# Attention and two gated products on one core: v for its norms loaded two squares ahead into buffers of its own, the fourth stage's results turned a quarter later

## The chip, the cores and the metric

The kernel runs on one core of a Trainium2 chip. A core has a matrix engine (TensorE, PE in the profile), a vector engine (DVE), a scalar engine (ACT), GpSimd (POOL), and SyncE (SP), which here issues all the large transfers; 16 DMA engines carry them. The metric is the device time of one execution in microseconds.

## What is computed

Float32 attention over 4 batches, 12 heads, 448 positions and 64 elements, whose result is 1792 rows of 768, and behind it two products in a chain (their weights come as float64):

```python
q_n, k_n = (rmsnorm(q, g_q), rmsnorm(k, g_k))
scores = scale * np.matmul(q_n, k_n.transpose(0, 1, 3, 2))
attn = np.exp(scores - max); attn = attn / (sum + 1e-09)
x = np.matmul(attn, v)               # then heads side by side: 1792 x 768
a = x @ w_a; b = x @ w_b             # 768 -> 1536
x = a * b @ w_out                    # 1536 -> 768
h = x @ w_in                         # 768 -> 2048
g = np.maximum(h, 0.0) + alpha * np.minimum(h, 0.0)
out = g @ w_out                      # 2048 -> 768
```

(The lines are shortened; the second product's weights are `moe2_w_in` and `moe2_w_out`.)

## The kernel before

Two streams of work are woven together by the code's order. The first is attention (`att_steps`): heads go in 24 pairs, six to a batch, and a pair in seven pieces of 64 queries of both heads; a step takes two pieces: scores `s` on TensorE, the maximum on DVE (L417), its scaling (L430) and the exponential (L434) on ACT, the probabilities as float16 high and low parts `p` on ACT and DVE (L479, L480), a transposing DMA `pT` on SP (L486), and after a pair's seven pieces the product with v (`x<-pT,v`). A pair is prepared ahead: `kr` and `qr` are loaded (L202, L206), squared for their norms (L232, L235), scaled, cast (L343, L341), transposed by DMA (`qT` L351, `kT` L354), and `qS`, qT with its halves exchanged, is copied from it (L357, L358). From batch 1 on TensorE's scores take qT first and qS after it.

The second stream is four matmul stages to a batch, `a`, `y`, `h` and `o`, in the order a0 y0 h0 o0 a1 y1 a2 h1 o1 y2 a3 h2 y3 o2 h3 o3. Each stage is a row of chains of matmuls into one of three PSUM buffers; between them the table `RATE` says how many attention steps are let in. On first use a piece of weights is loaded as raw float64 (L628), made float32 on ACT and DVE (L644, L647, L650), scaled and split to float16 parts `w` (L711, L712), used, and stored (L715, `sc_a` to `sc_o`); later batches load the stored parts (L624). So all conversion falls into a0 to o0, some 100 to 415 us.

Two places matter here. `vnorm(b, p)` squares v of a pair on ACT (L371) with the row sums in `ssv`; six of them are summed on TensorE by a matmul with ones (`tot<-ssv`) and give v's scale in a batch. Its buffer `vn` is loaded on the spot (L363), from a pool with two buffers, `ob`, that `finish` uses too. `stage_o` makes six chains of four quarters; `finish(m, ps)` takes a chain's result: ACT puts it from PSUM to `t` (L880), TensorE turns it in four transposes (L887), ACT scales it to `ob` (L889), SP stores it (L890). It is called behind the first quarter of the next chain, and for the last chain at once.

The code's order is a wish: a scheduler places each instruction in a queue for its engine by its own estimate, so that a small edit can change the order of many instructions behind it. Each engine then works through its queue in that order. The names in the rows are those of the program's tiles: `p<-g,w` is a matmul of stage o, `p<-x,w` of stage a.

Of the kernel before, what the change touches and what calls it, by code (L numbers as in the profile page):

```python
# [8 lines left out]
F32 = mybir.dt.float32  # L9
# [10 lines left out]
def attention_gated_mlps_kernel(  # L20
# [16 lines left out]
    B, H, S, D = q.shape  # L37
# [3 lines left out]
    NP = H // 2  # L41
    NI = S // 64
    KB = 4
    KP = S // KB
# [9 lines left out]
    ob_p = ctx.enter_context(tc.tile_pool(name="ob", bufs=2))  # L54
    in_p = ctx.enter_context(tc.tile_pool(name="in", bufs=2))
# [80 lines left out]
    def setup():  # L136
        for t, src in ((gT, g_q), (gkT, g_k)):
            for h in range(2):
                nc.sync.dma_start(
                    out=t[64 * h:64 * h + 64], in_=src.rearrange("(d o) -> d o", o=1)  # L140
                )
        make_identity(nc, ident)
        for t in qT0:
            nc.gpsimd.memset(t, 0.0)
        for t in stat:
            nc.gpsimd.memset(t, 1.0)

    def setup1():
        nc.gpsimd.tensor_tensor(gT, gT, gkT, op=ALU.mult)
        nc.gpsimd.tensor_scalar(gT, gT, float(D) ** -0.5, None, op0=ALU.mult)  # L150

    def setup0():
        nc.vector.memset(ones, 1.0)
        for t in p16:
            nc.vector.memset(t, 0.0)

    def setup2():
        nc.gpsimd.dma_start(out=gbc, in_=g_q.rearrange("(o d) -> o d", o=1).broadcast_to([128, D]))
        nc.gpsimd.dma_start(out=gkb, in_=g_k.rearrange("(o d) -> o d", o=1).broadcast_to([128, D]))
        nc.gpsimd.dma_start(out=al, in_=alpha.rearrange("(f p) -> p f", p=128))  # L160
# [35 lines left out]
    def load_qk(g):  # L196
        if g >= B * NP:
            return
        b, p = divmod(g, NP)
        qr = in_p.tile([128, NI, D], F32, tag="qr", name="qr")  # L200
        kr = in_p.tile([KP, 2 * KB, D], F32, tag="kr", name="kr")
        nc.sync.dma_start(  # L202
            out=kr.rearrange("p (h i) d -> p h i d", h=2),
            in_=k[b, 2 * p:2 * p + 2].rearrange("h (p i) d -> p h i d", i=KB),
        )
        nc.sync.dma_start(  # L206
            out=qr, in_=q[b, 2 * p:2 * p + 2].rearrange("h (p i) d -> (h p) i d", i=NI)
        )
        P[g]["qr"], P[g]["kr"] = qr, kr
# [15 lines left out]
    def prep0(g):  # L225
        if g >= B * NP:
            return
        d = P[g]
        st = stat[g // 2 % 2][:, g % 2]
        sq = one_p.tile([128, 2 * KB, D], F32, tag="sq", name="sq")[:, 0:NI]  # L230
        sk = one_p.tile([128, 2 * KB, D], F32, tag="sq", name="sk")[0:KP]
        i = nc.scalar.activation(out=sk, in_=d["kr"], func=AF.Square)  # L232
        if g in PIN1:
            tc.keep_in_program_order(i)
        nc.scalar.activation(out=sq, in_=d["qr"], func=AF.Square)  # L235
        i = nc.vector.reduce_sum(out=st[:KP, NI:NS], in_=sk, axis=AX.X)
        if g in PIN0:
            tc.keep_in_program_order(i)
        nc.vector.reduce_sum(out=st[:, 0:NI], in_=sq, axis=AX.X)
# [41 lines left out]
    def prep3f(g):  # L281
        prep3f_a(g)
        prep3f_b(g)
# [74 lines left out]
        nc.sync.dma_start(out=qS[64:128], in_=qT[0:64])  # L358
        d["qT"], d["kT"] = (qT, qS), kT

    def load_vn(b, p):
        vn = ob_p.tile([KP, 2, KB, D], F32, tag="ob", name="vn")
        nc.sync.dma_start(  # L363
            out=vn, in_=v[b, 2 * p:2 * p + 2].rearrange("h (p i) d -> p h i d", i=KB)
        )
        return vn

    def vnorm(b, p):
        vn = load_vn(b, p)
        sv = one_p.tile([128, 2 * KB, D], F32, tag="sq", name="sq")[0:KP]  # L370
        nc.scalar.activation(  # L371
            out=sv, in_=vn.rearrange("p h i d -> p (h i) d"), func=AF.Square,
            accum_out=ssv[:, b, p:p + 1],
        )

    def vscale(b):
        power(total(ssv[:, b], NP), sx[:, b:b + 1], ix[:, b:b + 1])
# [232 lines left out]
    for st in stages:  # L610
        n, parts, _ = CHAINS[st[0]]
# [128 lines left out]
    def next_w():  # L740
        u = cur[0]
        cur[0] += 1
        w16.pop(u)
        advance(u)
        if tasks:
            tasks.pop(0)()

    def unit():
        w = w16[cur[0]]
        return w.rearrange("p l (k f) -> p l k f", f=128)  # L750

    def prod(o, w, kk, x, first, last):
        hi, lo = w[:, 0, kk, :], w[:, 1, kk, :]
        mm(o, hi, x[:, 0], first, False)
        mm(o, hi, x[:, 1], False, False)
        mm(o, lo, x[:, 0], False, last)

    def new_ps():
        return ps_m.tile([128, 512], F32, tag="p", name="p")

    def tmp():
        return tmp_p.tile([128, S], F32, tag="t", name="t")
# [110 lines left out]
    def stage_o(b):  # L873
        NT, PT = 4, S // 4
        k = CHAINS["o"][2]

        def finish(m, ps):
            t = tmp()

            nc.scalar.activation(  # L880
                out=t.rearrange("q (p c) -> q c p", c=NI),
                in_=ps.rearrange("q (c p) -> q c p", c=NI),
                func=AF.Copy, scale=inv["o"][:, m:m + 1],
            )
            po = new_ps()[:PT].rearrange("p (t f) -> p t f", t=NT)
            for i in range(NT):
                nc.tensor.transpose(po[:, i, :], t[:, i * PT:(i + 1) * PT], ident)  # L887
            ob = ob_p.tile([PT, NT, 128], F32, tag="ob", name="ob")
            nc.scalar.activation(out=ob, in_=po, func=AF.Copy, scale=cum[:PT, b:b + 1])  # L889
            nc.sync.dma_start(  # L890
                out=out[b * S:(b + 1) * S, m * 128:(m + 1) * 128].rearrange("(t p) f -> p t f", t=NT),
                in_=ob,
            )

        c = cum[:, b:b + 1]
        nc.gpsimd.tensor_tensor(c, ix[:, b:b + 1], iab[:, b:b + 1], op=ALU.mult)
        nc.gpsimd.tensor_tensor(c, c, iy, op=ALU.mult)
        nc.gpsimd.tensor_tensor(c, c, icg, op=ALU.mult)
        nc.gpsimd.tensor_tensor(c, c, ix[:, b:b + 1], op=ALU.mult)
        late = None  # L900
        for m in range(KD):
            ps = new_ps()[:, 0:S]
            for part in range(4):
                yield
                hw = unit()
                for kk in range(k):
                    prod(
                        ps, hw, kk, G[b, part * k + kk],
                        part + kk == 0, part == 3 and kk == k - 1,
                    )  # L910
                if part == 0 and late:
                    finish(*late)
                next_w()
            late = (m, ps)
        finish(*late)
        for f in range(KF2):
            G.pop((b, f))
# [4 lines left out]
    if True:  # L922
        load_qk(0)
        setup()
        load_qk(1)
        setup0()
        prep0(0)
        setup1()
        prep3f(0)
        prep1((0,), NI, NS)  # L930
        prep2f(0)
        prep4f(0)
        prep0(1)
        prep1((0,), 0, NI)
        load_v(0)
        prep1((1,))
        load_v(1)
        load_qk(2)
        setup2()
        att = att_steps()  # L940
        n, done = 0, 0
        W0, EVERY = 4, 2
        while done < NP:
            g = [next(att) for _ in range(3)][-1]
            n += 1
            if n >= W0 and (n - W0) % EVERY == 0:
                advance((n - W0) // EVERY - 9 if n < 22 else -1)
            if n == 8:
                setup3()
                setup4()  # L950
            if g is not None:
                done += 1
        state["pin"] = False
        advance(-1)

        def step():
            nonlocal done
            done += next(att, None) is not None

        for i, st in enumerate(stages):  # L960
            s, b = st[0], int(st[1])
            if s == "a":
                while done < (b + 1) * NP:
                    step()
            n, parts, _ = CHAINS[s]
            ticks = n * parts
            gen = {"a": stage_a, "y": stage_y, "h": stage_h, "o": stage_o}[s](b)
            want, acc = 3 * RATE.get(st, 0), 0
            for _ in gen:
                acc += want  # L970
                while acc >= ticks:
                    acc -= ticks
                    step()
# [30 lines left out]
```

## Time and profile before

| | |
|---|---|
| median of 3 runs | 1224.51 us (1223.84 to 1224.89) |
| the profiled execution, and its span | 1225.36 us, 1223.6 us |
| mean granted TensorE clock | 0.985 |
| PE busy | 1158.7 us (95%) |
| ACT busy | 714.4 us (58%) |
| DVE busy | 673.7 us (55%) |
| POOL busy | 11.9 us (1%) |

The span is the time from the first to the last instruction that the profiler recorded on the core; the execution's time has a little around it. Shares are of the span. A busy share is a mean over stages that have different limits.

### The profile page before, as it was taken

What the parts mean: (1) busy time and instruction counts of PE and PEld (TensorE: products, weight loads), DVE (VectorE), ACT (ScalarE), POOL (GpSimd) and SP (SyncE); (2) the same over time, 40 slices, a digit from 0 to 9 for tenths busy, and PEclk for the clock granted to TensorE, in tenths of its full rate; (3) what the DMA queues carried; (4) which work ended last, traced back from release to release, by engine and by line L of the source; (5) the groups of instructions that cost most, each with busy time, mean ns of one, the idle gap of its engine ahead of it and who ended that gap; (6) DMA issues with size and microseconds to landing.
All of it is one profiled execution on the core that took longest, in us unless ns stands there. A gap on an engine that the chain in (4) does not pass through costs nothing.

```text
span 1223.6 us, 18095 instructions
## 1 busy us (share of the span) xinstructions
PE 1158.7 (95%) x6550; PEld 595.6 (49%) x6550; DVE 673.7 (55%) x1442; ACT 714.4 (58%) x1458; POOL 11.9 (1%) x32
## 2 busy tenths in 40 slices
PE   6997999889988899989999999999999999999998
PEld 3553554444434444445455445545555555554554
DVE  7898999999999767667542465332101440002400
ACT  7998999999999767675533465452111440113311
POOL 1000000000000000000000000000000000000000
PEclk9997999999999999999999999999999999999999
DMA  6558999999999999797854637876333333354343
GB/s 186 175 164 217 311 324 324 278 298 301 318 261 300 266 257 246 189 230 177 208 153 126 168 106 168 192 191 163 104 116 116 116 117 107 105 151 128 95 129 88
DMA packets 311241, 234.65 MB, mean 192 GB/s; under 512 B 175440, under 2 KB 284496, under 8 KB 311152
## 3 DMA queue, kind: packets, MB, share of 16 engines
q1 hardware_dynamic: 311040, 233.43, 71.8%
q8 instruction: 51, 0.84, 0.3%
q0 software_dynamic: 112, 0.07, 0.1%
q14 instruction: 38, 0.31, 0.1%
HBM read 155.79 MB, written 32.24 MB: 154 GB/s over the span
## 4 chain that ended last, share of the span: by engine, by line
PE 52%; DMA 1%; ACT 1%; DVE 1%; issue 0%; SPq 0%; ACTq 0%
PE p L108 48%; PE s L108 2%; PE x L108 2%; PE p L887 1%; DMA pT<-p 1%; DMA kr<-in_k_dram 0%; ACT t L880 0%; DMA qT<-q 0%; ACT pf L434 0%; ACT p L479 0%; DVE p L480 0%; DVE nm L417 0%; SPq L486 0%; DVE ab L788 0%; ACT x L530 0%
## 5 line engine op out<-in xcount | busy, mean ns | idle before, releaser
L108 PEld LDWEIGHTS <-w 128*128 128x128 f16 x4896 | 474.9, 99 | 466.9 <-issue 39.9
L108 PE MATMUL p<-x,w 128*128 128x448 f16 x1728 | 336.6, 354 | 0.3 <-DVE ab L788 0.2
L108 PE MATMUL p<-g,w 128*128 128x448 f16 x1152 | 228.1, 354 | 6.3 <-ACT g L847 2.2
L108 PE MATMUL p<-y,w 128*128 128x448 f16 x1152 | 222.3, 353 | 0.2 <-DVE t L862 0.2
L108 PE MATMUL p<-ab,w 128*128 128x448 f16 x864 | 169.5, 356 | 1.4 <-ACT ab L766 1.2
L417 DVE TENSOR_REDUCE nm<-s 128x2 f32<-128x896 f32 x84 | 91.2, 1085 | 38.3 <-PE s L108 38.2
L480 DVE SCALAR_TENSOR_TENSOR p<-pf,ri,p 128x448 f16<-128x448 f32 x126 | 84.1, 680 | 30.7 <-ACT p L479 30.5
L479 ACT ACTIVATE p<-pf,ri 128x448 f16<-128x448 f32 x126 | 81.2, 664 | 33.9 <-DMA pT<-p 25.8
L862 DVE SCALAR_TENSOR_TENSOR t<-t,al,p 128x448 f32<-128x448 f32 x55 | 37.3, 678 | 100.6 <-ACT t L861 100.5
L434 ACT ACTIVATE pf<-s,nm,esc 128x448 f32<-128x448 f32 x126 | 90.1, 719 | 1.4
L788 DVE SCALAR_TENSOR_TENSOR ab<-p,inv_a,t 128x448 f32<-128x448 f32 x48 | 32.5, 678 | 100.0 <-PE p L108 99.8
L880 ACT ACTIVATE t<-p,inv_o 128x448 f32<-128x448 f32 x24 | 25.6, 1065 | 81.5 <-PE p L108 81.5
L712 DVE SCALAR_TENSOR_TENSOR w<-wf,sc,w 128x768 f16<-128x768 f32 (+1 forms) x76 | 70.1, 928 | 3.0 <-ACT w L711 2.5
L791 ACT ACTIVATE junk<-ab 128x448 bf16<-128x448 f32 x48 | 27.6, 575 | 70.4 <-DVE ab L788 69.8
L711 ACT ACTIVATE w<-wf,sc 128x768 f16<-128x768 f32 (+1 forms) x76 | 65.5, 869 | 3.4 <-DMA sc_h<-w 1.7
L644 ACT ACTIVATE wf<-raw 128x768 f32<-128x768 f32 (+1 forms) x76 | 63.7, 843 | 4.6 <-DMA raw<-in_moe_w_in_dram 2.7
L650 DVE SCALAR_TENSOR_TENSOR wf<-raw,wf 128x768 int32<-128x768 int32 (+1 forms) x76 | 65.8, 867 | 0.3
L658 ACT ACTIVATE junk<-wf 128x768 bf16<-128x768 f32 (+1 forms) x76 | 59.2, 779 | 1.4 <-DVE wf L650 1.3
L861 ACT ACTIVATE t<-p 128x448 f32<-128x448 f32 x55 | 29.8, 542 | 48.0 <-PE p L108 47.9
L108 PE MATMUL s<-kT,qT 128*64 128x448 f16 x252 | 48.4, 376 | 9.2 <-DMA kT<-k 6.3
L847 ACT ACTIVATE g<-t,cgf 128x448 f16<-128x448 f32 x55 | 36.7, 668 | 34.6 <-DVE t L862 34.6
L848 DVE SCALAR_TENSOR_TENSOR g<-t,cgf,g 128x448 f16<-128x448 f32 x55 | 37.5, 682 | 29.5 <-ACT g L847 29.5
(137 smaller groups left out, 1030.5 us busy)
## 6 DMA issues: line engine op xcount, KB each, us to landing
w<-sc_a SPq DMA_DIRECT2D x72, 384.0 KB, 3.2
w<-sc_h SPq DMA_DIRECT2D x48, 384.0 KB, 3.1
w<-sc_o SPq DMA_DIRECT2D x72, 256.0 KB, 3.1
w<-sc_y SPq DMA_DIRECT2D x36, 384.0 KB, 3.2
raw<-in_moe_w_in_dram SPq DMA_DIRECT2D x16, 768.0 KB, 7.8
raw<-in_moe_w_out_dram SPq DMA_DIRECT2D x24, 512.0 KB, 6.3
raw<-in_moe_w_a_dram SPq DMA_DIRECT2D x12, 768.0 KB, 7.2
raw<-in_moe_w_b_dram SPq DMA_DIRECT2D x12, 768.0 KB, 6.4
```

Source lines behind the costliest of these rows:

```text
L108: nc.tensor.matmul(out=o, lhsT=a, rhs=b, start=first, stop=last)
L417: nc.vector.tensor_reduce(out=nm, in_=ps[:, :, 0:S], axis=AX.X, op=ALU.max, negate=True)
L434: nc.scalar.activation(out=pf, in_=ps[:, j, 0:S], func=AF.Exp, bias=nm[:, j:j + 1], scale=scale[j], accum_out=su[:, j:j + 1],)
L479: nc.scalar.activation(out=t[:, 0, :, 0:KP], in_=pf, func=AF.Copy, scale=r)
L480: nc.vector.scalar_tensor_tensor(out=t[:, 1, :, 0:KP], in0=pf, scalar=r, in1=t[:, 0, :, 0:KP], op0=ALU.mult, op1=ALU.subtract,)
L644: nc.scalar.activation(out=t, in_=hi.bitcast(F32), func=AF.Prelu, scale=2.0 ** -112, alpha=-(2.0 ** 32))
L650: nc.vector.scalar_tensor_tensor(out=ti, in0=lo, scalar=29, in1=ti, op0=ALU.logical_shift_right, op1=ALU.bitwise_or)
L658: nc.scalar.activation(out=junk(768, size(kind)), in_=t, func=AF.Square, accum_out=sums[0][:, j:j + 1])
L711: nc.scalar.activation(out=w[:, 0], in_=t, func=AF.Copy, scale=s)
L712: nc.vector.scalar_tensor_tensor(out=w[:, 1], in0=t, scalar=s, in1=w[:, 0], op0=ALU.mult, op1=ALU.subtract)
L848: nc.vector.scalar_tensor_tensor(out=x[:, 1], in0=t, scalar=cgf[:, f:f + 1], in1=x[:, 0], op0=ALU.mult, op1=ALU.subtract,)
L862: nc.vector.scalar_tensor_tensor(out=t, in0=t, scalar=al[:, f:f + 1], in1=ps, op0=ALU.mult, op1=ALU.add)
```

## The change

`vn` gets two buffers of its own in another pool (tag `vn` of `in_p`). The loads for the first two squares are issued at the end of the setup, and `vnorm` for pair n issues the load for pair n + 2 behind its square. In `stage_o` a chain's `finish` is called behind the second quarter of the next chain instead of the first.

```diff
-    def load_vn(b, p):
-        vn = ob_p.tile([KP, 2, KB, D], F32, tag="ob", name="vn")
+    vns = {}
+
+    def load_vn(n):
+        if n >= B * NP:
+            return
+        b, p = divmod(n, NP)
+        vns[n] = vn = in_p.tile([KP, 2, KB, D], F32, tag="vn", name="vn")
         nc.sync.dma_start(
             out=vn, in_=v[b, 2 * p:2 * p + 2].rearrange("h (p i) d -> p h i d", i=KB)
         )
-        return vn
 
     def vnorm(b, p):
-        vn = load_vn(b, p)
+        n = b * NP + p
+        vn = vns.pop(n)
...
             accum_out=ssv[:, b, p:p + 1],
         )
+        load_vn(n + 2)
...
-                if part == 0 and late:
+                if part == 1 and late:
                     finish(*late)
...
         load_qk(2)
+        load_vn(0)
+        load_vn(1)
         setup2()
```

Behind these lines the line numbers of the changed kernel are 5 to 8 higher: its L880 is L886, L711 is L717, L479 is L485, L371 is L376; L202 to L358 keep theirs. The scheduler's order stays the same on ACT, DVE and PE for the first 235 to 265 us and changes at many places from there to about 490 us. Three of them follow.

ACT at the end of o0, from the last preparation of a pair to the first attention step behind o0, before the change:

```order
L235 ACTIVATE sq<-qr 128x448
L530 ACTIVATE x_5_5165<-x 128x448
L385 ACTIVATE v_5486<-vr,sx 112x8x64
L232 ACTIVATE sk<-kr 112x512
L880 ACTIVATE t<-p,inv_o 128x7x64
L479 ACTIVATE p_0_108<-pf,ri 128x4x112
L889 ACTIVATE ob<-p,cum 112x512
L479 ACTIVATE p_1_109<-pf,ri 128x4x112
L235 ACTIVATE sq<-qr 128x448
L430 ACTIVATE nm<-nm,esc 128x2
```

The same place on ACT after the change, where L886 and L895 are the same two steps of `finish`:

```order
L235 ACTIVATE sq<-qr 128x448
L536 ACTIVATE x_5_5169<-x 128x448
L391 ACTIVATE v_5490<-vr,sx 112x8x64
L886 ACTIVATE t<-p,inv_o 128x7x64
L485 ACTIVATE p_0_108<-pf,ri 128x4x112
L895 ACTIVATE ob<-p,cum 112x512
L485 ACTIVATE p_1_109<-pf,ri 128x4x112
L232 ACTIVATE sk<-kr 112x512
L436 ACTIVATE nm<-nm,esc 128x2
```

The t of the last chain (L880, L886) now stands ahead of L232, the square of a kr, and no longer behind it.

ACT around the t of the fifth chain of o0 (`w_4971` to `w_5063` are the last pieces of o0's weights), before the change:

```order
L371 ACTIVATE sq,ssv<-vn 112x512
L479 ACTIVATE p_3_111<-pf,ri 128x4x112
L343 CAST k_5039<-kr 112x8x64
L430 ACTIVATE nm<-nm,esc 128x2
L434 ACTIVATE pf,su<-s,nm,esc 128x448
L880 ACTIVATE t<-p,inv_o 128x7x64
L711 ACTIVATE w_4971<-wf,sc 128x512
L711 ACTIVATE w_5004<-wf,sc 128x512
L711 ACTIVATE w_5026<-wf,sc 128x512
L889 ACTIVATE ob<-p,cum 112x512
L371 ACTIVATE sq,ssv<-vn 112x512
L711 ACTIVATE w_5063<-wf,sc 128x512
```

The same on ACT after the change; the first of the four pieces, `w_4975`, stands 4 rows further up:

```order
L717 ACTIVATE w_5008<-wf,sc 128x512
L485 ACTIVATE p_2_110<-pf,ri 128x4x112
L717 ACTIVATE w_5030<-wf,sc 128x512
L485 ACTIVATE p_3_111<-pf,ri 128x4x112
L341 CAST q_5041<-qr 128x7x64
L343 CAST k_5043<-kr 112x8x64
L717 ACTIVATE w_5057<-wf,sc 128x512
L436 ACTIVATE nm<-nm,esc 128x2
L886 ACTIVATE t<-p,inv_o 128x7x64
L440 ACTIVATE pf,su<-s,nm,esc 128x448 x2
```

The squares of vn (L371) that stood here have gone to earlier places, and all four pieces of weights stand ahead of this t.

SP where pair 11 is transposed, in o0 at 350 to 361 us, before the change:

```order
L351 DMA_TRANSPOSE qT<-q_4106 128x7x128
L486 DMA_TRANSPOSE pT<-p_2_110 128x8x128
L486 DMA_TRANSPOSE pT<-p_3_111 128x8x128
L715 DMA sc_o_0_3763<-w_4242 256x1x512
L354 DMA_TRANSPOSE kT<-k_4108 128x8x112
L357 DMA qS<-qT 64x896
L358 DMA qS<-qT 64x896
L202 DMA kr<-in_k_dram 112x2x256
L206 DMA qr<-in_q_dram 128x448
```

SP at the same place after the change:

```order
L492 DMA_TRANSPOSE pT<-p_2_110 128x8x128
L721 DMA sc_o_0_3767<-w_4246 256x1x512
L492 DMA_TRANSPOSE pT<-p_3_111 128x8x128
L351 DMA_TRANSPOSE qT<-q_4110 128x7x128
L354 DMA_TRANSPOSE kT<-k_4112 128x8x112
L202 DMA kr<-in_k_dram 112x2x256
L206 DMA qr<-in_q_dram 128x448
L357 DMA qS<-qT 64x896
L358 DMA qS<-qT 64x896
```

The transposing DMA qT went behind the two of pT, and the two copies qS behind the loads of kr and qr.

Two more places are told in words. At the front, SP issues two loads vn ahead of the first three raw weights (`raw`, L628) that stood behind these before. In o0, the loads vn 17 and 18 (counted from 0; at 405.69 and 412.93 us before) now stand where 15 and 16 stood (316.30 and 329.80 us), and 19 and 20, which stood at 451 us, stand where 17 and 18 were.

## Rows read from the trace of the kernel before

**Rows 1.** Windows of 20 us: each engine's busy time, TensorE's clock, DMA share, GB/s:

```profile
400.00:420.00 20.00, 18.52 (x110) 9.29 (x107) 14.28 (x34) 16.66 (x36) 0.00 (x0) 1.00 1.14 277
440.00:460.00 20.00, 20.00 (x126) 9.55 (x125) 13.73 (x26) 14.30 (x35) 0.00 (x0) 1.00 1.10 248
```

**Rows 2.** Timeline of PE at 410 to 415 us: start, duration, [idle before]:

```profile
410.46 0.39 PE L108 MATMUL tot<-ssv,ones 112*128 112x6 f32 x2 [0.62 <-ACT sq L371]
...
414.09 0.55 PE L108 MATMUL p<-g,w 128*128 128x448 f16 x2 [0.76 <-ACT w L711]
```

**Rows 3.** Timeline of ACT at 409 to 415 us:

```profile
409.69 0.63 ACT L371 ACTIVATE sq<-vn 112x512 f32<-112x512 f32 x1 [2.29 <-DMA vn<-in_v_dram]
...
410.88 0.60 ACT L343 CAST k<-kr 112x512 f16<-112x512 f32 x1
...
412.49 1.07 ACT L880 ACTIVATE t<-p,inv_o 128x448 f32<-128x448 f32 x1
413.36 1.90 ACT L711 ACTIVATE w<-wf,sc 128x512 f16<-128x512 f32 x3
```

**Rows 4.** Timeline of PE at the end of o0:

```profile
428.69 0.57 PE L108 MATMUL s<-kT,qT 128*64 128x448 f16 x4 [1.64 <-DMA kT<-k]
431.18 0.65 PE L887 MATMUL p<-ident,t 128*112 128x128 f32 x4 [1.92 <-ACT t L880]
```

**Rows 5.** Timeline of ACT at the end of o0:

```profile
429.54 0.63 ACT L232 ACTIVATE sk<-kr 112x512 f32<-112x512 f32 x1 [3.75 <-DMA kr<-in_k_dram]
430.08 1.05 ACT L880 ACTIVATE t<-p,inv_o 128x448 f32<-128x448 f32 x1
```

**Rows 6.** Timeline of SP's queue (SPq) at 421 to 426 us: issue times, not transfers:

```profile
421.51 1.40 SPq L351 DMA_TRANSPOSE qT<-q  x1
422.96 2.64 SPq L354 DMA_TRANSPOSE kT<-k  x1
425.65 0.76 SPq L202 DMA_DIRECT2D kr<-in_k_dram  x1
```

**Rows 7.** Windows of 2 us, columns as in the first group:

```profile
260.00:262.00 2.00, 2.00 (x12) 0.88 (x9) 0.69 (x2) 2.00 (x3) 0.00 (x0) 1.00 0.95 193
432.00:434.00 2.00, 2.00 (x8) 0.65 (x5) 0.95 (x2) 1.69 (x3) 0.00 (x0) 0.57 0.88 324
434.00:436.00 2.00, 2.00 (x8) 0.72 (x8) 1.20 (x2) 0.07 (x1) 0.00 (x0) 0.57 0.96 244
692.00:694.00 2.00, 2.00 (x10) 0.67 (x10) 1.54 (x3) 1.12 (x3) 0.60 (x2) 0.50 1.18 238
```

**Rows 8.** Waits of ACT: us in total, times, longest:

```profile
ACT sq L371 <- DMA vn<-in_v_dram: 8.3, 6, 3.0
```

**Rows 9.** Timeline of PE in o1, at 812 to 822 us:

```profile
812.77 0.65 PE L887 MATMUL p<-ident,t 128*112 128x128 f32 x4 [0.41 <-ACT t L880]
...
814.23 6.98 PE L108 MATMUL p<-g,w 128*128 128x448 f16 x36
```

**Rows 10.** Timeline of PE at two idle times elsewhere:

```profile
259.01 0.38 PE L108 MATMUL s<-kT,qT 128*64 128x448 f16 x2 [2.55 <-DMA kT<-k]
...
690.24 0.39 PE L108 MATMUL tot<-ssab,ones 128*128 128x12 f32 x2 [1.76 <-ACT junk L791]
```

**Rows 11.** Timeline of SP's queue at 24 to 28 us:

```profile
24.02 0.45 SPq L628 DMA_DIRECT2D raw<-in_moe_w_a_dram  x1
...
25.76 2.20 SPq L363 DMA_DIRECT2D vn<-in_v_dram  x2
```

**Rows 12.** The page's DMA issues: count, KB each, median us to landing:

```profile
raw<-in_moe_w_a_dram SPq DMA_DIRECT2D x12, 768.0 KB, 7.2
```

**Rows 13.** Timeline of ACT at 36 us:

```profile
36.68 1.72 ACT L644 ACTIVATE wf<-raw 128x768 f32<-128x768 f32 x2
```

**Rows 14.** Timeline of SP's queue where pair 11 is transposed:

```profile
350.87 1.25 SPq L351 DMA_TRANSPOSE qT<-q  x1
353.60 2.61 SPq L486 DMA_TRANSPOSE pT<-p  x2
...
359.57 0.58 SPq L202 DMA_DIRECT2D kr<-in_k_dram  x1
360.21 0.49 SPq L206 DMA_DIRECT2D qr<-in_q_dram  x1
```

## The prediction

> **What bounds the kernel now.** I read the page's busy times first, then the windows of 20 us, then for every TensorE idle of more than 0.2 us the timelines of PE, ACT and SP around it. TensorE is the engine that ends last: it is busy for 95% of the span, and from 440 us on a window shows it full, 20.00 of 20 [rows 1]. So what can be won is TensorE's idle time ahead of 440 us, and little behind it. The change touches o0 (360 to 431 us), where TensorE has 1.5 us idle in the 20 us from 400 on, while ACT and DVE are busy for 16.66 and 14.28 of them and the DMA engines show a share of 1.14 [rows 1]: there neither vector engine is the bound, the DMAs are. Four idle times count.
>
> At 410.46 TensorE waits 0.62 us for the sum of the norms' squares, at 414.09 0.76 us for a weight piece w [rows 2]. Behind both stands one stall of ACT, which works in program order: it sat 2.29 us until vn had landed, squared it at 409.69, and so came late to the next t (L880, 412.49) and the three pieces of w behind it (413.36) [rows 3]. At 428.69 TensorE waits 1.64 us for a transposed k (kT), and after 0.57 us of work again 1.92 us, at 431.18, for t of the last chain of o0 [rows 4]. That t starts on ACT at 430.08 only, because L232, in front of it, needs a kr whose load SP had issued at 425.65 [rows 5, 6]. Right after it TensorE's granted clock falls: 0.57 in both windows from 432 to 436 us, with TensorE busy 2.00 of 2 in each [rows 7].
>
> **The change, part by part.**
>
> *The squares.* ACT's waits for vn come to 8.3 us in 6 times [rows 8]. With each load two squares ahead of its use they go: in the new order of SP the load 17 stands about where the load 15 stood. What that is worth to TensorE is not 8.3: behind 440 us it is full anyway, so the waits there are worth nothing, and if that cover were gone they would hold scores, not matmuls. Of the waits in o0 TensorE sees the 0.62 and the 0.76 = 1.38 us. In the order after the change the squares 17 and 18 stand some 13 us earlier and the four last w of o0 ahead of the t of chain 4, so both reasons are gone.
>
> *But 1.38 us is not yet a gain.* TensorE must still wait for the kT at 428.69, and who sets that? Its data were cast at 410.88 [rows 3], and SP issued qT and kT at 421.51 and 422.96 [rows 6], some 10 us later. SP was not waiting for data: its 33 issues from 394.91 to 425.65 follow one another with one gap of more than 0.15 us, as the rows at 421.51, 422.96 and 425.65 show (each starts 0.05 us behind the end of the one before) [rows 6]. After the change the same things stand ahead of this kT on SP from that point on: two vn loads (17, 18) are gone, two later ones (19, 20) are there instead. So kT lands where it did, TensorE comes to it 1.38 us sooner, and waits 1.64 + 1.38 = 3.02 us. I take 0 for the two waits; the other end is the full 1.38, if SP should be sooner, and a further 1.64 if kT ceases to be waited for.
>
> *The last chain of o0.* The 1.92 at 431.18 stand behind that kT, so nothing that comes later on TensorE's side takes them up: t (L880, now L886) has moved ahead of the L232 with its late kr, its psum is complete when TensorE leaves for the scores, and the 3.02 us at kT cover its 1.05 us [rows 5]. That is -1.92. It could be lost only if ACT is late at that t for another reason; ahead of it stand L235, L536 and L391, none of which waits for the moved load. L232 now stalls ACT behind it: on SP its kr load goes behind two transposes pT and two copies qS, an estimated 4 us later (2 x 1.40 as for the qT at 421.51, 2 x 0.58 as for a load [rows 6, 14]). Queued behind it on ACT are a scale of maxima, an exponential and the first t of the next stage; TensorE has three psum buffers and is full from then on, so I cost this at 0, and at up to its 2 us if that cover is too thin.
>
> *The transposes of finish, a quarter later* (12 matmuls, at 36 in 6.98 us 2.3 us [rows 9]). In o0 this and the new order balance: for the chain at 387 us ACT's t moves back nearly as far. In o1 the one wait of 0.41 us inside the stage, at 812.77 [rows 9], goes: 2.3 us cover it. The finishing call of each stage doesn't move. -0.41, between 0 and -0.41.
>
> *The clock at 432 us.* It took 2 windows x 2.00 us x (1 - 0.57) = 1.72 us [rows 7]. Before, 3.56 us of idle in 4.13 went ahead of it; afterwards it would be 3.02 us in one piece. Other places don't settle what such a gap does: after 2.55 us of idle at 259.01 I see no fall, after 1.76 us at 690.24 there is one (0.50 in the window from 692) [rows 7, 10]. 3.02 lies half-way between 2.55 without and 3.56 with, so I take half, -0.86, with both ends, 0 and -1.72, in the range. The Trainium skill ("TensorE: Matmul & The Clock Gate", Part 1, on the HAM clock gate) says that the hardware's monitor runs free of the kernel, so that the place of a transition varies from run to run. That the shorter of these two gaps is the one with a fall agrees with it; by that rule alone the fall would be a matter of phase, and could stay at the full price, which is the first rival.
>
> *The front of the kernel.* Two vn loads (2.20 us of SP with what they wait for) now stand ahead of the first three raw weights [rows 11]. These are issued some 3.9 us later, at about 27.9 instead of 24.0, and with the 7.2 us to landing that the page gives [rows 12] arrive near 35.1, ahead of their use on ACT at 36.68 [rows 13]: 0, with only 1.6 us to spare.
>
> *The sum.* 0 - 1.92 - 0.41 - 0.86 = -3.19 us. The profiled execution took 1225.36 us (1223.6 of span, the rest around it), which gives 1222.2; the median of the runs is 0.85 lower, 1224.51, so the forecast is 1221.3 us.
>
> **The rivals.**
>
> *A. The clock falls as before.* Only 1.92 + 0.41 = 2.33 are won: 1222.2 us. For it: the fall at 690.24 after a smaller gap [rows 10].
>
> *B. All of it.* SP gets to the kT as much sooner as ACT does, the 1.38 is kept, the gap stays at 1.64 and the clock holds: -0.62 - 0.76 - 1.92 - 1.72 - 0.41 = -5.43, 1219.1 us; with the kT's own 1.64 as well, 1217.4. Against it: SP's unbroken rows.
>
> *C. It does nothing.* The vn loads 19 and 20, which stood behind 440, now go ahead of that kT, so the program moves two loads more before it. Each is 112 x 512 x 4 bytes; both, 0.46 MB, take 1.7 us at the 277 GB/s of the window [rows 1]. If the DMAs have been the bound all the way from 217 us, where the first load was moved to, kT lands that much later and 2.33 becomes about 0.7: 1223.8 us. For it: the share of 1.14. Against it: SP idles between 348 and 354 us (the qT issued at 350.87 is over by 352.1, and the next row is at 353.60 [rows 14]), so not the whole way is bound. The Trainium skill ("Trainium Kernel Development and Optimization", Key Constraints) says that all queues run on the same 16 DMA engines and interleave; by it an earlier load is a load taken from others. No row here shows that for vn.
>
> *D. Slower, by SP's order at pair 11.* In the order after the change the two copies qS of that pair stand behind qT, kr and qr: 1.25 + 0.58 + 0.49 = 2.3 us later [rows 14]. TensorE would stand still for up to 2.3 us more and could see the clock fall once more, 1.7: +4.0. Eight more matmuls stand ahead now (1.5 us), and the idle times up to 428.69 could take up the rest; what ACT and DVE still take from TensorE is late if they do not. It decides where the loss reaches the kT at 428.69: +4.0 with the gain of 2.33 held, 1226.2; with it lost as well, 1228.5.
>
> **How the numbers follow.** The forecast with its half clock and A are one mechanism, 0.50 together (0.25 with the clock held or in part, 0.25 as A); B 0.17, C 0.18, D 0.15. 0.2% of 1224.5 is 2.45 us, about what a measurement of this kernel can tell from no change: under 1222.06 is faster, over 1226.96 slower. Faster: B, the clock's better half, and half of A, which lies on the line, 0.54. Slower: most of D, 0.12. The same: 0.34. The range leaves out B's far end and most of D: 1217.5 to 1226.0 us. The likeliest case's own range is 1220.5 to 1222.6.
>
> **What would show it.** Right: no ACT wait for vn in o0; no TensorE wait for w or the sum of squares at 405 to 420; a wait for kT of about 3 us near 426, and none for t behind it; the windows after it at a clock of 1.00 or 0.57, which tells the forecast from A. Wrong: a kT wait that stays at 1.6 (B), one of over 4 us (C), or idle of more than 2 us near 360 for qS (D). The forecast as a whole would be wrong if the time of o0 were set by ACT or DVE rather than by SP's queue.

## The result, and the profile after

The change makes the kernel slower: 1232.17 us (median of 9 runs, 1228.27 to 1235.75) against 1224.89 us before (1223.07 to 1226.78); the ratio is 1.0053, with a 95% interval of 1.0036 to 1.0070. The forecast was 1221.3 us, faster. The profiled execution took 1232.93 us, its span is 1231.2. (A ratio here is the one on record over the runs of both kernels; it need not be the quotient of the two medians.) One execution of a kernel further down, own buffers with the finish part, took 5200.31 us at a granted clock of 0.223 and is left out of that kernel's numbers.

To find the place I compare when TensorE starts the same matmul in the two traces (us from the span's start; worked out from the timelines of PE):

```
                              before    after   difference
first matmul of a1             431.7    434.2        +2.5
matmul 216 of a1 (of 432)      486.2    487.8        +1.6
matmul 252 of a1               494.0    497.5        +3.5
matmul 288 of a1               501.8    508.6        +6.8
matmul 360 of a1               519.9    529.6        +9.7
first matmul of y1             547.2    556.7        +9.5
first matmul of o3            1160.5   1168.1        +7.6
```

So most of the loss arises within 35 us of stage a1, behind the place where the forecast stops looking. The page's row of TensorE has hardly changed (95% before):

```profile
PE 1160.4 (94%) x6550; PEld 597.2 (49%) x6550; DVE 673.8 (55%) x1442; ACT 713.8 (58%) x1458; POOL 11.7 (1%) x32
```

The windows of the kernel before, columns as in [rows 1]. TensorE is full in each of them, as in the one from 440 on:

```profile
460.00:480.00 20.00, 20.00 (x118) 9.57 (x118) 16.00 (x37) 13.12 (x30) 0.00 (x0) 1.00 1.10 264
480.00:500.00 20.00, 20.00 (x126) 9.69 (x122) 13.32 (x24) 15.03 (x38) 0.00 (x0) 1.00 1.01 230
500.00:520.00 20.00, 20.00 (x124) 9.81 (x123) 15.23 (x37) 12.32 (x31) 0.00 (x0) 1.00 0.65 171
```

The kernel after: from 480 us on TensorE is no longer full, and in the window from 500 on its mean clock is down:

```profile
460.00:480.00 20.00, 20.00 (x122) 9.55 (x119) 8.57 (x16) 9.56 (x22) 0.00 (x0) 1.00 1.08 230
480.00:500.00 20.00, 18.16 (x114) 8.90 (x113) 16.77 (x38) 14.56 (x35) 0.00 (x0) 1.00 0.73 184
500.00:520.00 20.00, 16.93 (x83) 7.51 (x83) 11.24 (x27) 12.77 (x30) 0.00 (x0) 0.83 0.97 228
```

The row of 460 to 480 us shows DVE and ACT falling behind: they are at 8.57 and 9.56 where they had 16.00 and 13.12 before, while TensorE is still full, on what they had prepared. ACT alone waits 4.42 us there, for a kr of pair 17 that was issued 5.4 us later than before. The timeline of PE after, the end of o0 (which answers to [rows 4]) and then a1:

```profile
426.06 2.46 PE L108 MATMUL x<-pT,v 112*64 112x448 f16 x24 [1.65 <-DMA pT<-p]
...
433.26 0.54 PE L108 MATMUL s<-kT,qT 128*64 128x448 f16 x3 [1.86 <-DMA kT<-k]
433.73 0.65 PE L893 MATMUL p<-ident,t 128*112 128x128 f32 x4
...
497.52 3.57 PE L108 MATMUL p<-x,w 128*128 128x448 f16 x18 [1.84 <-DVE ab L794]
...
508.60 6.49 PE L108 MATMUL p<-x,w 128*128 128x448 f16 x18 [2.96 <-DVE ab L794]
```

TensorE needs a free PSUM buffer, and `ab` (L788 before, L794 now) is what frees it. The product that `ab` reads has long been summed, but DVE works in program order, and in front of `ab` stand instructions that wait for a late pair. Now back along the chain. SP's queue after (qr of pair 17 is the row at 476.79, kr of 17 the one at 462.67):

```profile
462.67 0.57 SPq L202 DMA_DIRECT2D kr<-in_k_dram  x1
...
476.79 0.57 SPq L206 DMA_DIRECT2D qr<-in_q_dram  x1
...
489.65 0.33 SPq L206 DMA_DIRECT2D qr<-in_q_dram  x1
...
490.55 0.38 SPq L202 DMA_DIRECT2D kr<-in_k_dram  x1
...
502.11 1.35 SPq L354 DMA_TRANSPOSE kT<-k  x1
```

and SP's queue before:

```profile
457.27 0.57 SPq L202 DMA_DIRECT2D kr<-in_k_dram  x1
457.90 0.45 SPq L206 DMA_DIRECT2D qr<-in_q_dram  x1
...
492.92 1.25 SPq L354 DMA_TRANSPOSE kT<-k  x1
```

Before, qr of pair 17 was issued at 457.90, 0.06 us behind the kr; the new order has put it behind seven transposes pT (the last is pT 55), 14 us behind the kr. SP's longest wait from 470 to 500 us (us in total, times, longest), after and then before:

```profile
SPq L206 <- DVE q L349: 6.6, 1, 6.6
SPq L202 <- DVE k L352: 1.5, 1, 1.5
```

ACT after:

```profile
479.60 0.58 ACT L235 ACTIVATE sq<-qr 128x448 f32<-128x448 f32 x1 [1.72 <-DMA qr<-in_q_dram]
...
488.21 0.55 ACT L341 CAST q<-qr 128x448 f16<-128x448 f32 x1
...
494.19 0.63 ACT L232 ACTIVATE sk<-kr 112x512 f32<-112x512 f32 x1 [2.44 <-DMA kr<-in_k_dram]
...
506.61 0.62 ACT L343 CAST k<-kr 112x512 f16<-112x512 f32 x1 [3.10 <-DMA kT<-k]
```

and DVE after:

```profile
489.00 0.62 DVE L349 TENSOR_TENSOR q<-qr,q 128x448 f16<-128x448 f32 x1
...
494.85 0.69 DVE L236 TENSOR_REDUCE stat<-sk 112x8 f32<-112x512 f32 x1 [1.55 <-ACT sk L232]
...
496.79 0.68 DVE L794 SCALAR_TENSOR_TENSOR ab<-p,inv_a,t 128x448 f32<-128x448 f32 x1
...
507.25 0.69 DVE L352 TENSOR_TENSOR k<-kr,k 112x512 f16<-112x512 f32 x1 [3.09 <-ACT k L343]
507.86 0.68 DVE L794 SCALAR_TENSOR_TENSOR ab<-p,inv_a,t 128x448 f32<-128x448 f32 x1
```

Pairs 16 and 17 share the computing of their norms (L254 and on), so the late q of 17 holds up 16 too. q of 16 is cast at 488.21 and read by DVE until 489.62; that frees its buffer, and 0.03 us later, at 489.65, SP can issue the load of q of pair 18 into it. SP, which works in order too, has stood still for this buffer for 6.6 us, and what stands behind is late. k of 18 stands behind that load (490.55; its own buffer, read by DVE's L352 until 490.22, was not free much sooner), ACT's L232 waits for it, DVE's `stat` waits for L232, and `ab` at 496.79 stands behind `stat` (and behind a p that waited 0.65 us more). Then it happens a second time: the kT of the pair ahead is issued at 502.11, 9.2 us later than before, the cast of k (L343) waits 3.10 us until this kT has been read out of the one buffer k16, DVE's L352 waits for the cast, and `ab` at 507.86 stands behind. The second gap also costs clock. Windows of the kernel after:

```profile
508.00:510.00 2.00, 1.40 (x4) 0.56 (x4) 1.54 (x2) 1.06 (x4) 0.00 (x0) 0.50 1.06 260
510.00:512.00 2.00, 2.00 (x7) 0.85 (x6) 0.34 (x2) 1.51 (x5) 0.00 (x0) 0.50 1.03 364
512.00:514.00 2.00, 2.00 (x7) 0.82 (x6) 1.39 (x2) 2.00 (x4) 0.00 (x0) 0.50 1.03 388
```

At half speed (a granted clock of 0.50 in place of 1.00) these three windows lose 0.5 x (1.40 + 2.00 + 2.00) = 2.7 us. With 1.84 + 2.96 that is 7.5 of the 8.1 us by which the difference grows between matmuls 216 and 360 of a1.

### The profile page after: what moved, and what is told of

Same layout as the page of the kernel before. It is cut to its first block, busy times and chain, and to the rows that moved or that the text cites. A ratio compares the mean times of both kernels' runs of the same rounds, so it can differ in the third digit from the quotient of the medians.

```text
span 1231.2 us, 18095 instructions
## 1 busy us (share of the span) xinstructions
PE 1160.4 (94%) x6550; PEld 597.2 (49%) x6550; DVE 673.8 (55%) x1442; ACT 713.8 (58%) x1458; POOL 11.7 (1%) x32
## 4 chain that ended last, share of the span: by engine, by line
PE 54%; ACT 1%; DVE 0%; DMA 0%; issue 0%; SPq 0%; ACTq 0%
PE p L108 50%; PE s L108 2%; PE x L108 2%; PE p L893 1%; ACT pf L440 0%; DMA pT<-p 0%; ACT t L886 0%; PE tot L108 0%; ACT junk L797 0%; DVE nm L423 0%; ACT x L536 0%; DVE v L392 0%; DVE p L486 0%; ACT p L485 0%; SPq L492 0%
## 5 line engine op out<-in xcount | busy, mean ns | idle before, releaser
L485 ACT ACTIVATE p<-pf,ri 128x448 f16<-128x448 f32 x126 | 81.0, 663 | 36.9 <-DMA pT<-p 29.8
L794 DVE SCALAR_TENSOR_TENSOR ab<-p,inv_a,t 128x448 f32<-128x448 f32 x48 | 32.5, 678 | 97.6 <-PE p L108 97.5
L717 ACT ACTIVATE w<-wf,sc 128x768 f16<-128x768 f32 (+1 forms) x76 | 65.0, 863 | 2.6 <-DMA sc_o<-w 1.3
L886 ACT ACTIVATE t<-p,inv_o 128x448 f32<-128x448 f32 x24 | 25.6, 1065 | 61.9 <-PE p L108 61.9
```

The source lines that it names most:

```text
L485: nc.scalar.activation(out=t[:, 0, :, 0:KP], in_=pf, func=AF.Copy, scale=r)
L717: nc.scalar.activation(out=w[:, 0], in_=t, func=AF.Copy, scale=s)
```

## The experiments

The theory (T1): the loss is the late load of q of pair 17, which the scheduler's new order put behind pT 53 to 55. The rivals: the earlier loads in a full DMA or o0's new order (T2); the later turn of `finish` (T3). Each kernel was timed in five rounds beside the kernel before.

**The last three loads on the spot.** Everything as in the changed kernel, but:

```diff
     def vnorm(b, p):
         n = b * NP + p
+        if n not in vns:
+            load_vn(n)
         vn = vns.pop(n)
...
-        load_vn(n + 2)
+        if n + 2 < 21:
+            load_vn(n + 2)
```

> The changed kernel, but the last three loads of vn (21 to 23) are issued on the spot again. TensorE's order stays that of the changed kernel in every row; SP differs in rows 330 to 353, ACT in 661 to 691, DVE in 945 to 989, all in stage a1: the load of q of pair 17 goes back from behind the transposes pT 53 to 55 to its place right behind that of k. Theory T1 (the loss sits in a1: late q of pair 17, squares and buffers late behind it, ACT and DVE blocked in order): the waits of 1.84 and 2.96 us for ab and the half clock behind them (3.4 us), 8.1 us together, go: about 1224 us, no loss against before. Rival T2 (the loss comes from o0, or from the earlier loads in a full DMA): nothing changes, about 1232 us.

Measured: 1223.94 us against 1224.24 before, ratio 0.9987 (0.9973 to 1.0001). The whole loss is gone, as T1 said, with TensorE's order untouched. Against T2: this kernel has all of o0's new order and the early loads up to 20. Windows of this kernel:

```profile
480.00:500.00 20.00, 20.00 (x120) 9.55 (x117) 13.23 (x24) 14.95 (x35) 0.00 (x0) 1.00 0.98 194
500.00:520.00 20.00, 20.00 (x124) 9.80 (x123) 15.24 (x37) 12.64 (x31) 0.00 (x0) 1.00 0.70 205
```

**The late load alone, put into the kernel before.** In `load_qk`:

```diff
+        if g == 17:
+            i = nc.sync.dma_start(out=qr, in_=...)
+            tc.keep_in_program_order(i)
         nc.sync.dma_start(out=kr..., in_=...)
-        nc.sync.dma_start(out=qr, in_=...)
+        if g != 17:
+            nc.sync.dma_start(out=qr, in_=...)
```

> The kernel before, with one thing changed: the load of q of pair 17 is pinned on SP behind the transposes pT 53 to 55, where the changed kernel has it. TensorE's order is that of before in every row; SP differs in 7 rows, ACT in 27, DVE in 46, all in a1. T1 (that late load is the loss): the stall of a1 comes, two waits of some 1.8 and 3 us for ab near 488 and 500 us and the half clock behind them, 1224.2 + 8.1 = about 1232 us. T2 (the loss needs the earlier loads of vn or o0's new order): no change, 1224 us.

Measured: 1230.89 us against 1225.21, ratio 1.0054 (1.0037 to 1.0071): the loss of the changed kernel (1.0053), without an early load of vn and with o0's old order. T2 falls with it, and T1 holds from both sides. One limit remains: in both runs the scheduler moved more along with the load. On SP a vn load went ahead, vr went behind the transposes and k of 18 behind q of 18; 30 to 36 rows of ACT and 46 of DVE in a1 changed. The load and the order that comes with it are shown as one thing. The profiled execution is the fastest of this kernel's five (1227.52 us, span 1225.7); it has the second of the two waits, and the clock behind it. PE, and SP's longest wait from 470 to 500 us:

```profile
502.58 2.77 PE L108 MATMUL p<-x,w 128*128 128x448 f16 x7 [2.15 <-DVE ab L794]
```

```profile
SPq L212 <- DVE q L355: 7.4, 1, 7.4
```

and its clock:

```profile
504.00:506.00 2.00, 2.00 (x7) 0.83 (x6) 0.34 (x2) 1.51 (x5) 0.00 (x0) 0.53 1.02 337
```

**The part on vn alone** (`if part == 0 and late:` put back).

> Only the part on vn: own buffers, loads two squares ahead; finish stays behind the first quarter. In its order the loads of both k and q of pair 17 stand behind pT 53 to 55. T1: the stall in a1 is there as in the changed kernel, or worse (k is late too): about 1232 us or more. Rival T3 (the later turn of finish is what costs): no loss, 1222 to 1225 us.

Measured: 1234.02 us against 1224.24, ratio 1.0072 (1.0052 to 1.0092). As T1 said; T3 falls as the whole cause, since `finish` is where it was. PE of this kernel has most of the stall in one piece:

```profile
503.79 5.25 PE L108 MATMUL p<-x,w 128*128 128x448 f16 x18 [3.98 <-DVE ab L794]
```

**The part on finish alone** (before, with `if part == 1 and late:`).

> Only the part on finish: the result is turned behind the second quarter; vn is loaded on the spot into the shared buffers. In its order q of pair 17 stands behind pT 53 and q of pair 18 ahead of its k, half of what the changed kernel has. T1: a part of the loss in a1, 0 to 8 us; the waits for vn remain: 1222 to 1232 us. T3: the whole loss, about 1232 us.

Measured: 1226.62 us against 1224.24, ratio 1.0016 (1.0001 to 1.0031). It doesn't touch vn at all, and yet its trace (of the slowest of its twelve executions, 1230.41 us) has the stall of a1, for its order too has q of 17 behind five pT, up to pT 53:

```profile
495.01 3.57 PE L108 MATMUL p<-x,w 128*128 128x448 f16 x18 [1.38 <-DVE ab L788]
...
506.19 2.03 PE L108 MATMUL p<-x,w 128*128 128x448 f16 x5 [3.06 <-DVE ab L788]
```

So neither edit "does" the damage; each makes the scheduler find another order, and with either of them, as with both, the load is late.

**Own buffers, loaded on the spot** (before, with `vn` from `in_p`, tag `vn`), and **the same with the finish part**. The first keeps the orders of before in a1, the second has q of 17 behind its k:

> Before with buffers of its own for vn, everything else as it was; the orders in a1 on SP are those of before. It tells whether a shared buffer was part of the waits for vn. T1: no loss, 1222 to 1225 us; a gain only if the loads waited for results' buffers, the vn loads in o0 (2.29 and 0.51 us of ACT's wait) being where it would show.

> The finish part of the change with buffers of its own for vn, but no early loads. In its order q of pair 17 stands right behind its k, unlike with the finish part alone. T1: no stall in a1; the last chain's wait for t at the end of o0 (1.92 us) and the small waits of o1 (0.4 to 0.7 us) stay away: 1221 to 1224 us, the best of these kernels. T3 (turning later costs by itself): about 1226.6 us, as the finish part alone.

Measured: 1224.40 us against 1224.24, ratio 0.9998 (0.9987 to 1.0010), and 1224.08 us against 1224.16, ratio 0.9998 (0.9984 to 1.0011). The traces give no sign that the shared buffer was part of the waits: ACT's waits for vn in the first are not shorter (12.2 us in 7 times, 8.3 in 6 before [rows 8]). The second kernel shows that turning later need not cost anything; against the finish part alone (1.0016) it has q of 17 in its place, but its order differs at other places too. The gain that I expected is not there. In its trace TensorE is 3.9 us ahead of the kernel before at matmul 72 of a1 and level with it at matmul 396, and the lead goes in small waits:

```profile
500.30 3.56 PE L108 MATMUL p<-x,w 128*128 128x448 f16 x18 [0.90 <-DVE ab L788]
...
524.38 3.56 PE L108 MATMUL p<-x,w 128*128 128x448 f16 x18 [1.39 <-ACT t L785]
```

The first kernel, with the order of before on every engine but for three rows of ACT, goes from 3.5 us ahead to 1.0: in a1 a lead from o0 is partly waited off even where q of 17 is in its place.

**The part on vn alone, last three loads on the spot.**

> The part on vn alone (finish behind the first quarter), with the last three loads on the spot, so that q of pair 17 stands right behind its k. T1: the loss of the vn part alone (9.8 us) goes, and what it won in o0 stays: in the trace of the vn part alone the first matmul of a1 came 5.8 us earlier than before, so 1219 to 1222 us. T2: about 1234 us as the vn part alone. A third theory (all of o0's gain is taken back by SP's queue whatever the order): 1224 us.

Measured: 1228.73 us against 1225.21, ratio 1.0025 (1.0012 to 1.0038). 0.47 of the 0.72% went, as T1 said, but the gain in o0 that I expected is not there; it is still slower than before. Its trace begins a1 2.8 us ahead of the kernel before and is 2.5 us behind at matmul 72 and still at matmul 360. Between stands a longer wait for kT, with a clock of 0.50 behind it from 434 to 438 us:

```profile
433.64 0.58 PE L108 MATMUL s<-kT,qT 128*64 128x448 f16 x2 [3.44 <-DMA kT<-k]
```

So in this trace there is no stall at q of 17, and the rest of the loss comes from this wait; no run tells why the kT is late here.

**One square ahead** instead of two (`load_vn(n + 1)`, one load at setup).

> The changed kernel with vn loaded one square ahead instead of two. In its order q of pair 17 stands right behind its k. T1: no stall in a1; o0 ordered in another way again, 1220 to 1225 us. T2: as the changed kernel, about 1232 us.

Measured: 1225.63 us against 1225.21, ratio 1.0000 (0.9987 to 1.0012). Early loads cost nothing here and bring nothing that can be measured.

**Stores off SP** (the first kernel of this section, `nc.gpsimd.dma_start` for the 24 stores of o0's weights).

> The first of these kernels (last three loads on the spot), with the 24 stores of o0's weights issued from GpSimd's queue instead of SP's. It tests whether SP's issuing is what makes TensorE wait for pT (2.16 us) and kT (2.47 us) at the end of o0. If so, both waits shrink: up to 4.6 us and the half clock behind them (1.7) less than 1223.9, 1218 to 1221 us. If the DMA engines themselves are the bound, the waits stay: about 1224 us. The order changes in o0 and a1, so the waits in the profile decide, not the time alone.

Measured: 1232.61 us against 1225.21, ratio 1.0054 (1.0033 to 1.0074). My expectation failed. This loss is another one than T1's: q of 17 is in its place, and TensorE begins a1 8.9 us late and loses about 1 us more in it. At the end of o0 the wait for kT is gone, one for pT of 1.56 us stays, but a new one comes earlier. PE and SP of this kernel:

```profile
405.10 0.53 PE L108 MATMUL s<-kT,qT 128*64 128x448 f16 x1 [5.83 <-DMA kT<-k]
```

```profile
393.79 0.37 SPq L637 DMA_DIRECT2D raw<-in_moe_w_out_dram  x1
394.32 3.13 SPq L351 DMA_TRANSPOSE qT<-q  x1
397.56 3.32 SPq L354 DMA_TRANSPOSE kT<-k  x1
```

SP took 3.13 and 3.32 us over two issues whose median is 1.3 us, with fewer issues in the queue. But such long ones are not new: before, 24 of the 162 transposing issues took over 2 us (2.64 for the kT in [rows 6]). This kT ended TensorE's wait only 7.5 us after its issue, the one of [rows 6] 5.7 us after [rows 4]. So fewer issues on SP did not help; that the transfers themselves are held up would fit but is not shown, since the order changed too.

**Inside the chain of the stall.** Two kernels take one link each out of the late-q kernel: k of 18 pinned ahead of q of 18, and two buffers for k16 (`two_p` instead of `one_p`). A third gives the two buffers to the finish part alone.

> The kernel before with the late q of pair 17 as in the run before, but the load of k of pair 18 stands ahead of that of q of pair 18 again. TensorE's order stays that of before. It splits the chain of the stall. If the costly link is that k of pair 18 queues on SP behind a load of q whose buffer isn't free (SP idle for 6.7 us in the changed kernel, then ACT's 2.44 us for this k), its first wait, for ab at about 497 us, goes, and of some 6 us of loss about half or more: 1225 to 1228 us. If the late q itself is what costs (its squares and casts late, and what stands behind them in order), the loss stays: about 1231 us.

> The kernel before with the late q of pair 17, and with two buffers instead of one for k16, the cast k that the transposing DMA kT reads. TensorE's order and SP's order at pair 17 stay those of the late-q run. If what blocks ACT and DVE at about 500 us is the cast of k waiting for that one buffer (2.8 us, with ab behind it in order), the waits for ab there go and most of the loss with them: 1224 to 1227 us. If the late squares and loads are enough by themselves, the loss stays: 1229 to 1232 us.

> The finish part of the change alone, with two buffers for k16. TensorE's order is that of the finish part alone. If the single k16 buffer is the link, the waits for ab of 1.4 and 3.1 us in a1 go: 1221 to 1224 us, faster than before. If not, 1226 us as the finish part alone.

Measured: 1228.32 us against 1224.16, ratio 1.0038 (1.0022 to 1.0053); 1233.64 us against 1224.34, ratio 1.0069 (1.0048 to 1.0091); 1229.19 us against 1224.34, ratio 1.0038 (1.0024 to 1.0053). What the first link is worth can't be told: its interval overlaps that of the late-q kernel (1.0037 to 1.0071). Its trace says why the change is small. SP stands still all the same, now ahead of the load of k of 18, whose buffer pair 16 also had to leave:

```profile
SPq L207 <- DVE k L360: 6.1, 1, 6.1
```

In the traces of all runs SP's longest wait from 470 to 500 us is 5.9 to 8.1 us where q of 17 stands behind pT 55, 3.2 and 3.5 where it stands behind pT 53, and at most 3.0 where it stands right behind its k. That link the kernels with the stall have in common; no run took it out alone. The second link, k16, is not needed for the loss: with two buffers the wait near 502 us has gone, and the lateness comes out further on, in three other waits. PE of the late-q kernel with two buffers:

```profile
515.93 3.57 PE L108 MATMUL p<-x,w 128*128 128x448 f16 x18 [1.37 <-DVE ab L794]
...
530.82 5.25 PE L108 MATMUL p<-x,w 128*128 128x448 f16 x18 [2.18 <-ACT t L791]
549.41 0.38 PE L108 MATMUL s<-kT,qT 128*64 128x448 f16 x2 [2.17 <-ACT pf L440]
```

Here removing one place where the late pair shows moved the waits. (ACT's order changed in over 200 rows with the two buffers, so a part of this may be another order again. The finish part with two buffers lost time too; its profiled execution, span 1223.9, is not like its median, so its trace explains nothing.)

## Why the prediction was wrong

*The step that failed* is in "The squares" and "The last chain of o0": "behind 440 us it is full anyway, so the waits there are worth nothing", and for the stretch behind o0 "TensorE has three psum buffers and is full from then on, so I cost this at 0". A full window was read as slack. It tells that TensorE did not wait in this order; it doesn't tell how near its feeders were. DVE before:

```profile
488.69 0.68 DVE L788 SCALAR_TENSOR_TENSOR ab<-p,inv_a,t 128x448 f32<-128x448 f32 x1
...
497.24 0.68 DVE L788 SCALAR_TENSOR_TENSOR ab<-p,inv_a,t 128x448 f32<-128x448 f32 x1
```

These two `ab` end 4.6 and 3.9 us ahead of the matmuls 252 and 288 of a1 (494.0 and 501.8) that need their buffers. The new order made them 8.1 and 10.6 us later, more than that cover. I followed the moved instructions to the end of o0 only, although the order differs to about 490 us; the moved load of q stood in it, and none of the rivals looks behind o0. What the runs show in its place: the load of q of 17 14 us behind its mate, with the order that comes with it, costs 0.54%, where I had put 0.

*The waits of o0* were read rightly, but o0 did not become shorter without them. ACT's waits for vn went from 8.3 us to 0.6 [rows 8]; the waits at 410 and 414 us [rows 2] are gone; the t of the last chain is no longer waited for (433.73 above, 1.92 us before [rows 4]). In o1 0.3 us of waiting for t are left of 0.41 and 0.28. And yet, from the first matmul of o0 to matmul 72 of a1, TensorE took 111.1 us before and 111.5 after, where the forecast's terms up to there make 2.8 us less. In the other traces it took 109.8 with the same order in o0 (the last three loads on the spot) and 108.8 to 114.3 with the order of before (own buffers on the spot, the late-q kernel and its two variants): no gain stands out of this spread.

*The 1.38 us* that I held back did not become a gain, as said, but I had one transfer too few in view: instead of kT going from 1.64 to 3.02 us, TensorE waits 1.65 for pT and 1.86 for kT, 3.51 together. In the new order SP issues the pair's last two pT at 419.45 and 422.45 with a store of weights between them and more stores in front; before, they went out in one piece at 413.51. The prediction has no term for this. Nor did the kT "land where it did": SP issued it at 428.32, and at 423.98 in the kernel with the last three loads on the spot, against 422.96 [rows 6]. Whether SP or the DMAs set this is open (stores off SP).

*Pair 11* (rival D) got later: TensorE waits 2.28 us for its kT (1.09 before) and 0.42 for qS, where [rows 14] made me expect up to 2.3 more for qS. It was not what made the kernel slower: the kernel with the last three loads on the spot has the same order there and is not slower.

*The clock at 432 us* stayed at 1.00 after the change; in the kernel with the last three loads on the spot it fell to 0.57 at 430, behind a wait of 2.47 us for kT. The half price was a guess between two ends, and these two traces show one each. What I left out is that a new wait elsewhere brings its own: 2.7 us behind the wait at 508.60, more than a third of the loss.

*The front of the kernel* was read rightly: the raw loads went out at 27.77 us, and their use on ACT began at 36.83 (36.68 before [rows 13]).

*The sum.* With the a1 stall taken out, 0.13% is left (0.9987, an interval of 0.9973 to 1.0001 that includes no change): about 1.6 us where 3.19 were forecast, and not clear of nothing.

## What to carry to other kernels

A busy engine is no proof of slack: before you cost a moved instruction at nothing, ask how early its result comes in the trace (here 3.9 and 4.6 us), and follow every engine's moved rows to where the two orders meet again. In a queue that works in order, one load a few places later can hold up work that has nothing to do with it, by way of a buffer that isn't freed. Where a scheduler sets the order, test an edit once with its order and once with the old order pinned where they differ; here the difference between the two (0.66% between 0.9987 and 1.0053) was five times what the edit itself seemed to win.

## What was not expected of the hardware

The granted clock did not follow the length of the gap alone: in the traces of before and after it stayed at 1.00 behind 2.55 us [rows 7, 10] and 1.86 us of idle, and fell to 0.50 behind 1.76 [rows 7, 10] and 2.96. And the time that SP spends on issuing a transposing DMA varies much: before, its median is 1.3 us, but 24 of 162 took over 2 us and the longest 5.1. With 24 stores moved from SP's queue to GpSimd's it was no shorter (median 1.3 us, 34 of 162 over 2 us).
